# A fused attention and maxout kernel: unit 0's q and k in fp32 by Sync's queue, row maxima and crossbar transposes from unit 2 on, last two tiles as 64-row pairs, a new order table

## The chip, the cores and the metric

The kernel runs on one core of one Trainium2 chip. The metric is device time in microseconds (us) of one execution. Before the change three runs gave 293.11, 294.73 and 296.16 us, median 294.73. Profiles show one execution; its times count from the span's start.

## The reference

Inputs are `q`, `k`, `v` of shape (8 batches, 8 heads, 576 rows, 64), `w_phi` (64 x 128), three weights `w1`, `w2`, `w3` (512 x 768) and `w_out` (768 x 512), all float32. What is computed:

```python
def phi(x):
    proj = einsum('bhsd,df->bhsf', x, w_phi)
    proj = proj - max(abs(proj), axis=-1, keepdims=True)
    return concatenate([exp(proj), exp(-proj)], axis=-1)
q_p, k_p = phi(q), phi(k)
kv  = einsum('bhsf,bhsd->bhfd', k_p, v)
z   = sum(k_p, axis=2)
num = einsum('bhsf,bhfd->bhsd', q_p, kv)
den = einsum('bhsf,bhf->bhs', q_p, z)[..., None] + 1e-06
x   = (num / den) as (batch*row, head*dim)          # 4608 x 512
out = maximum(maximum(x @ w1, x @ w2), x @ w3) @ w_out
```

## The kernel before, in words

**Units.** Attention is cut into 16 units of four heads, half a batch each (`attention(u)`, L437 on). A unit's 4 x 576 rows stand as 18 tiles of 128 columns by two head pairs: tiles 0 to 8 and 9 to 17, of which 8 and 17 are "the last two tiles". In the work of one unit, by the letters that the code gives to its steps:

- L: q, k and v are loaded. For units 0 to 3 (`BY_PE`) POOL issues DMAs that cast q and k to bf16 on the way; only unit 0's k comes in fp32 by Sync's queue (`K0_SP`, L446 to L457), in two halves that VectorE casts. From unit 4 on q and k come in fp32 by Sync and GpSimd casts them.
- T: q and k are transposed, so that q has partitions 0 to 63 and k 64 to 127 of `qkT`: on TensorE for units 0 to 3 (L491), by one DMA crossbar transpose from unit 4 on (L506).
- G: the projections with `w_phi` (L521 to L534). Tiles in groups of four are done as 64-row matmuls, q and k as a pair of instructions side by side in the array (L533), into one PSUM bank each; the last two tiles as one 128-row matmul each, q and k side by side in 256 columns of one bank (L528). From unit 2 on (`JOIN`) two groups of four stand in one step.
- Maxima of the absolute values by VectorE (L552) and exponentials of k by ScalarE (L546).
- R, mT, V (from unit 4 on, `SUBT`): the maxima of q are transposed on TensorE (L560), copied, and written by a small DMA as row 64 of `qkT`, so that the second projection M subtracts them with a row of -1 in its weights (L613). For units 0 to 3 (`by_product`) M adds 34 small products with a negated identity instead (L618).
- K: `kv` from exponentials and scaled v, as 64-row matmuls (L642). N: the numerators and denominators (L660), divided by VectorE into `x_sb` (L666, L667).
- X: x is transposed into `xT`. For units 0 to 5 (`X_PE`) by ten TensorE transposes (L680) and two copies (L683), from unit 6 on by one DMA crossbar transpose on Sync's queue (L690).

**Chunks.** The second part runs by `chunk` (L697): eight chunks of 512 tokens, one for each batch, and a ninth of the 8 x 64 rows left over. `w1` is subtracted from `w2` and `w3`, and `w1 @ w_out` is made once (L814), so a chunk has 12 "up" steps of 4 matmuls (L713) and, for each of four row tiles, 4 matmuls with that product (L741) and 6 with `w_out` (L746), an evacuation (L754) and a store (L761). Chunk b needs the X steps of units 2b and 2b+1.

**Order.** Nothing is scheduled at run time. Every step is a node; the string `PLAN` lists, for each node, its number, its engine (T, D, A, G, S for PE, DVE, ACT, POOL, SP), the buffers that it gets, and a start time by which `fill` (L269) sorts the nodes. Each engine then runs its instructions in that order, and an engine whose next instruction waits lets nothing pass. Where `PLAN` leaves gaps on PE, `fill` puts matmuls without use ("idler", L846) that keep PE busy. There are eight PSUM banks, written out in `PLAN` too.

Of the kernel before, what the change touches and what calls it, by code (L numbers as in the profile page):

```python
# [16 lines left out]
DF = 128  # L17
# [24 lines left out]
X_PE = 6  # L42
SUBT = 4
# [3 lines left out]
JOIN = 2  # L47
# [4 lines left out]
K0_SP = 1  # L52
GATES = (None, (0, 0), (1, 0), (2, 0))
V_ACT = 4
# [48 lines left out]
47A0@17.5 63A@17.6 56A@18.1 54A@18.6 49G@14.6 45G@15.7 1054G@16.8 1062D0@14.4 46G@17.6 51G@18.7 50G@19.0 1052G@20.1
84D1@15.6 1066D@15.7 86T4@16.4 90T6@16.9 88T3@17.1 87D1@17.2 89D@17.8 91D@18.4 92T110211@18.0 102T41@18.6 97T35@18.8
112T6@19.1 95D@18.6 96D@19.3 107T70@19.4 103A@19.1 113A@19.6 93A@20.0 108A@20.5 109A@21.1 85S@15.8 105D@19.9 110D@20.5
67T047@21.2 115D@21.1 100D@21.4 106D@22.0 94A@21.6 98A@22.1 104A@22.8 68A@23.3 128T31@22.3 1063T2@22.8 222G0@20.9
159T1@23.4 131T4@24.0 129A@23.7 116D@22.6 69D@23.0 111D@23.3 121A1@24.2 114A@24.4 123G1@24.6 124G@25.7 101D@24.0
137T7@24.6 130A@24.7 139A@25.2 117A@25.6 99A@25.8 138A@26.3 118G@26.0 119G@27.1 122G@28.2 125T0@24.8 132A@26.6
133A@27.3 120A@27.8 134T6@25.3 136A@27.9 135A@28.6 126A@29.0 127A@29.7 223G@29.3 76T30@25.8 1053G@30.2 1057G@31.0
1055G@33.1 1064D@24.6 160D2@25.7 74T2@26.1 70T5@26.5 77D0@26.3 71D1@27.0 75D0@27.6 1071T1@26.8 157D2@28.3 1072D@28.4  # L110
158S@28.5 165T00735400@28.1 161T2@28.7 163T1@29.2 169D@29.0 164D@29.6 168D@29.8 172D@30.4 162D@31.0 166A@30.2
167A@30.8 1073T6@29.3 140T110@30.7 173D@31.6 174T7532@31.9 182D@32.6 1074A@31.3 141A@32.1 181D@33.2 177D@33.8
183T6@32.3 142A@32.5 185A@32.9 180A@33.3 179A@34.0 1069T1@32.7 170A@34.5 1070A@35.0 72T0@34.0 149T31@34.3 178D@34.4
187D@35.0 186D@35.5 188A0@35.5 175A@35.7 191A0@36.2 1067T7@34.6 190G@35.9 189G@38.0 1068A@36.4 1056G@40.1 150D1@35.8
143T2@35.9 80T1@36.2 147T3@36.6 145T7@37.0 144D0@36.5 224D3@37.1 73D1@37.2 146D0@37.8 148D1@38.4 225S@37.3 356S1@38.0
355S0@38.6 359G1@43.2 358G@44.7 201T20@37.4 176A@36.9 184A@37.4 195T5@37.8 192T6@38.3 171A@37.7 81D@39.0 202A@38.2
203A@38.8 290S0@40.3 151T0@38.8 78T4@39.1 153T7@39.4 152D@39.5 1060D@40.2 154D@40.8 79D@41.3 204T3@39.7 226T2@40.0
207T010@40.5 193A@39.3 205A@40.2 206A@40.7 197A@41.0 228T3@41.6 230T7@42.2 227D0@41.7 194A@41.5 196A@42.0 208A@42.5
198T4@42.3 209D@42.3 229D@42.7 232T11625011@42.9 1097T1@43.5 1085T3@44.4 199A@43.1 234A@43.7 231D@43.3 239D@43.7
236D@44.4 212T70@45.3 235D@45.0 233A@45.1 289S1@42.9 293G2@46.7 292G@49.1 1086A1@45.6 200A@46.1 213D0@45.9 360S1@46.0  # L120
1098D@46.5 237A@46.6 1081T5@45.6 250T6@46.5 241T2374@46.7 253D@47.1 244D@47.6 1058D@48.2 248D@48.8 1082A@47.1
247A@47.6 243A@48.1 252A@48.6 238A@48.9 1079T1@47.3 1080A@49.4 251A@49.9 1077T5@48.3 1083T2@49.1 242A@50.2 1078A@50.7
421S0@50.6 1084A@51.2 1089T7@50.0 249D@49.4 254D@50.4 240D@50.7 1090D@51.4 245D@52.0 1059D@52.6 265T11@50.9 262T6@51.4
271T5@51.8 273A@52.3 246A@52.7 272A@53.2 210T0@52.1 214T2@52.4 211D1@53.2 215D0@53.8 1087T7@52.7 1093T3@53.6
216T4@54.5 548S1@51.2 294S2@52.5 422S0@57.8 547S1@58.4 357S0@59.7 266A@53.5 263A@54.0 267A@54.5 268T5@54.8 218T0@55.3
255A1@55.0 264A@55.2 219A@55.8 1099T2@55.6 259T1@56.4 258A1@56.5 257G@55.4 256G@57.5 269A@56.6 260A@57.2 261A@57.8
270A@58.3 1094D@54.7 217D1@55.3 1088D@56.0 1100D@56.7 291S1@61.2 1397G@59.5 361T00364000@56.9 368D@57.7 364D@58.4
1095T7@57.5 1091T2@58.5 1096D@59.0 1092D@59.6 369D@60.2 370T1453@59.3 362A@58.8 375A@60.2 1101T7@59.9 367A@61.0
363A@61.5 379T2@60.9 378D@60.8 377D@61.4 382D@62.0 373D@62.4 381A@62.5 376A@62.9 365D@63.0 383D@63.6 374D@63.9
1102T@61.1 1105T5@62.4 1106T@63.3 384T1@64.6 1103A0@63.3 380A@64.1 274T136@64.6 1107D1@64.8 387A0@64.7 385A0@64.9  # L130
424G0@59.9 366A@65.2 390A0@65.7 550G1@66.5 425G@67.6 295T11721511@66.0 300A@66.7 297A@67.2 388G@68.7 389G@70.8
386S@65.3 275D@66.0 298D@66.7 276D@67.3 281T01@66.5 1109T3@67.0 296A@67.9 372A@68.4 301A@68.9 371A@69.3 283T7@67.9
279T6@68.2 282D0@67.7 284D1@68.4 280D0@69.1 1110T@68.5 1111A2@70.1 299D@69.7 1113T0@69.8 302D@70.3 303D@70.9
304T7642@70.7 305A@71.5 277T3@71.3 307D@71.5 278D1@72.1 311D@72.7 426S0@68.9 484S0@71.8 394T10@71.7 423S2@72.4
396A@72.2 395A@72.8 1114T@71.9 313T5@73.2 1115A3@73.5 220T7@73.4 287T3@73.7 611S0@73.7 610S1@75.2 486S3@76.6 317D@73.7
221D@74.0 308D@74.5 285T1@74.0 286A@74.6 310A@75.3 306A@75.7 288D@75.1 406T040@74.4 391T7@75.5 403T1@75.8 404A@76.2
309A@76.6 405A@77.1 407D@75.7 408D@76.1 312D@77.2 316D@77.8 1125T3@75.9 397T4@76.8 1119T6@77.0 1131T0@77.9 1120D0@78.2
399A@77.4 398A@78.0 392A@78.5 393A@79.2 315A@79.6 318T1@78.8 1132D@79.0 319D1@79.6 321A1@80.0 314A@80.2 324G1@80.4
320S@80.0 551G@80.7 1104S@80.7 411T20@78.8 487G2@81.8 1126A@80.6 1117T4@79.1 1129T6@80.0 1127T0@80.9 400T7@81.8
1118A@81.1 1128A@82.0 322G@82.9 323G@85.0 402A@82.5 401A@83.1 1130D@81.7 412D0@82.3 1139T1@82.0 1140D@83.1  # L140
436T00534600@82.8 1121T0@83.4 442A@83.7 441A@84.3 437A@84.8 438A@85.4 439D@83.7 443D@84.3 444D@84.9 427T2715@84.5
434D@85.5 440D@86.2 430D@86.8 433A@85.9 1122A@86.4 1123T4@85.1 1137T6@86.0 445T1@86.9 325T31@87.1 447A@87.4 326A@87.7
1124A@88.2 1135T0@87.4 1145T2@88.2 327A@88.7 448D@87.9 1138D@88.2 449D@88.8 446A@89.3 450T4@89.1 1133T6@89.2
1136D@89.2 451D0@89.8 331T3@90.0 328T1@90.2 432A@89.7 428A@90.2 429A@90.8 330A@91.3 435D@90.3 1134D@90.9 340T104@90.5
332A@91.8 341A@92.3 342D@91.9 431D@92.2 1149T5@91.6 1150T@92.6 1151D0@94.1 329A@92.7 453A0@93.1 333A@93.4 334T6@93.9
613G0@87.1 335A@94.3 336A@95.0 552S1@82.2 485S1@85.1 553T11407111@94.1 571T3@94.7 614G@88.2 575D@95.2 557D@95.6
560D@96.2 1146T@95.0 454G0@93.5 488G@95.6 574D@96.8 674S0@89.5 675S0@90.1 559A@95.5 558A@96.1 555A@96.6 556D@97.1
561D@97.7 572A@97.3 1108S@90.7 1116S@91.9 337T5@96.3 1141T6@96.4 1152S@94.9 549S1@96.1 1142T@97.3 1147A1@97.6
# [144 lines left out]
def kernel(  # L293
# [11 lines left out]
):  # L305
    nc = tc.nc

    try:
        from concourse.hw_specs import get_activation_tables
        _tables = list(get_activation_tables(nc.m.arch).keys())  # L310
        _set_id = _tables.index("natural_log_exp_and_others")
# [58 lines left out]
    def by_pairs(t):  # L370
        return t.rearrange("p (pr c) d -> p pr (c d)", c=NT)
# [506 lines left out]
```

## Time and profile before

| | |
|---|---|
| runs | 293.11, 294.73, 296.16 us |
| span of the profiled execution | 290.6 us |
| its whole time | not listed; the runs lie 2.5 to 5.6 us above the span |
| PE busy | 279.4 us, 3602 matmuls |
| DVE, ACT, POOL busy | 215.9, 189.9, 117.4 us |
| granted TensorE clock | 1.000 |
| HBM read, written | 34.67 MB, 9.44 MB |

The profile lists busy time for each engine; PE is matmuls, PEld loads of weights, which overlap them. A matmul's duration in a row is its way through the pipeline and not its price: the price is the step from its start to the next one's start. SPq, ACTq and POOLq rows are DMAs being issued. "DMA share" is the mean busy share of the 16 DMA engines; it is summed over packets and can pass 1.00 a little.

### The profile page before, as it was taken

How to read it: one execution, taken by the hardware profiler on the slowest of the kernel's cores; microseconds unless marked ns; L12 is line 12 of the kernel's file. 1: busy time of each engine (PE TensorE's matmuls, PEld its weight loads, DVE VectorE, ACT ScalarE, POOL GpSimd, SP SyncE). 2: the span in 40 equal slices, each digit the busy share in tenths (PEclk: the TensorE clock that was granted, in tenths of full speed). 3: DMA queues.
4: the chain of work that ended last, by engine and by line, in shares of the span. 5: the costliest groups of instructions: out<-in, count | busy, mean ns of one | idle time of the engine just before them, and what ended most of it. 6: DMA issues, size and time to landing. Idle time of an engine off the chain costs nothing.

```text
span 290.6 us, 8659 instructions
## 1 busy us (share of the span) xinstructions
PE 279.4 (96%) x3602; PEld 158.7 (55%) x3641; DVE 215.9 (74%) x457; ACT 189.9 (65%) x438; POOL 117.4 (40%) x101
## 2 busy tenths in 40 slices
PE   8878999999999999999999999999999999999993
PEld 3556685646645585564466556545555564444442
DVE  2987999998876899768989959898796583242360
ACT  1599798977988899799669797566858631120101
POOL 8086886276093751552780519107064300000000
PEclk9999999999999999999999999999999999999999
DMA  7999988997967799796995779658534523500605
GB/s 191 208 201 181 218 249 271 230 335 178 356 132 258 221 189 279 165 287 130 298 182 106 173 235 206 138 126 174 102 107 95 112 21 72 126 18 2 144 18 128
DMA packets 63051, 49.87 MB, mean 172 GB/s; under 512 B 43556, under 2 KB 48036, under 8 KB 63012
## 3 DMA queue, kind: packets, MB, share of 16 engines
q1 hardware_dynamic: 58644, 44.04, 61.2%
q0 software_dynamic: 4288, 5.21, 11.0%
q8 instruction: 28, 0.46, 0.6%
q14 instruction: 11, 0.09, 0.1%
q10 hardware_dynamic: 80, 0.07, 0.1%
HBM read 34.67 MB, written 9.44 MB: 152 GB/s over the span
## 4 chain that ended last, share of the span: by engine, by line
PE 86%; DVE 6%; ACT 4%; DMA 2%; issue 1%; SPq 0%; ACTq 0%
PE ups L713 30%; PE ops L746 16%; PE ops L741 11%; PE kvps L642 7%; PE psn L660 6%; PE psq L533 5%; PE psm L613 4%; DVE mqp L552 2%; DMA wphi_f<-in_w_phi_dram 2%; DVE mk L552 2%; ACT Ek L546 2%; PE tps L491 1%; PE pxT L680 1%; PE psm L618 1%; PE psq L528 1%
## 5 line engine op out<-in xcount | busy, mean ns | idle before, releaser
L588 POOL TENSOR_TENSOR vab<-v_raw,em 128x1152 bf16<-128x1152 f32 (+1 forms) x36 | 68.2, 1907 | 88.7 <-ACT em L584 67.7
L713 PE MATMUL ups<-xT,w_bf 128*128 128x512 bf16 x411 | 100.7, 379 | 1.1
L546 ACT ACTIVATE Ek<-psk 128x512 bf16<-128x512 f32 x128 | 70.5, 607 | 23.7 <-PE psk L533 17.0
L626 ACT ACTIVATE Eq<-psm 128x512 bf16<-128x512 f32 (+1 forms) x160 | 79.2, 586 | 7.9 <-PE psm L613 6.2
L713 PEld LDWEIGHTS <-w_bf 128*128 128x128 bf16 x432 | 40.3, 98 | 44.1 <-DVE x_sb L667 0.2
L746 PE MATMUL ops<-wout_bf,hT 128*128 128x512 bf16 (+1 forms) x219 | 50.7, 373 | 0.3
L552 DVE TENSOR_REDUCE mqp<-psq 128x4 bf16<-128x512 f32 (+1 forms) x80 | 47.7, 631 | 2.0 <-PE psk L533 1.0
L719 DVE TENSOR_TENSOR hT<-hT,ups 128x512 bf16<-128x512 bf16 x54 | 35.9, 683 | 14.2 <-ACT hT L721 6.8
L552 DVE TENSOR_REDUCE mk<-psk 128x4 f32<-128x512 f32 x64 | 42.5, 681 | 1.7 <-ACT Ek L546 1.2
L746 PEld LDWEIGHTS <-hT 128*128 128x128 bf16 x222 | 21.3, 98 | 22.8 <-DVE hT L719 0.2
L721 ACT ACTIVATE hT<-ups 128x512 bf16<-128x512 f32 x28 | 16.4, 613 | 26.2 <-PE ups L713 26.1
L667 DVE TENSOR_TENSOR x_sb<-psn,rden 128x320 bf16<-128x320 f32 x64 | 31.5, 492 | 2.2
L660 PEld LDWEIGHTS <-Eq 128*128 128x128 bf16 x640 | 24.5, 97 | 6.5 <-issue 0.3
L754 DVE COPY osb<-ops 128x512 f32<-128x512 f32 (+1 forms) x19 | 12.6, 674 | 18.9 <-PE ops L746 18.9
L660 PE MATMUL psn<-kv_sb,Eq 128*128 128x65 bf16 x640 | 26.3, 193 | 0.1
L723 DVE TENSOR_SCALAR hT<-ups 128x512 bf16<-128x512 f32 x26 | 17.5, 686 | 11.4 <-PE ups L713 11.1
L754 ACT COPY osb<-ops 128x512 f32<-128x512 f32 (+1 forms) x18 | 10.3, 575 | 23.7 <-DMA out_dram<-osb 9.6
L741 PE MATMUL ops<-xT 128*128 128x512 bf16 x86 | 24.1, 380 | 0.5
L642 PEld LDWEIGHTS <-Ek 64*128 64x128 bf16 x1152 | 18.4, 94 | 5.7 <-issue 2.8
L642 PE MATMUL kvps<-vab,Ek 64*128 64x65 bf16 x1152 | 20.5, 190 | 0.9 <-POOL vab L588 0.5
L533 PE MATMUL psq<-w,qkT 64*128 64x128 bf16 x256 | 20.4, 217 | 0.4 <-DVE qkT L494 0.4
L533 PEld LDWEIGHTS <-qkT 64*128 64x128 bf16 x512 | 14.5, 94 | 10.7 <-issue 7.7
(72 smaller groups left out, 277.8 us busy)
## 6 DMA issues: line engine op xcount, KB each, us to landing
v_raw<-in_v_dram SPq DMA_DIRECT2D x16, 576.0 KB, 4.6
out_dram<-osb SPq DMA_DIRECT2D x70, 128.0 KB, 2.4
k_raw<-in_k_dram SPq DMA_DIRECT2D x12, 576.0 KB, 4.9
q_raw<-in_q_dram SPq DMA_DIRECT2D x12, 576.0 KB, 6.1
w_bf<-in_moe_w_dram POOLq DMA_DIRECT2D x3, 768.0 KB, 10.0
qk_bf<-in_q_dram POOLq DMA_DIRECT2D x3, 288.0 KB, 10.6
qk_bf<-in_k_dram POOLq DMA_DIRECT2D x3, 288.0 KB, 11.1
wout_bf<-in_moe_w_out_dram POOLq DMA_DIRECT2D x1, 768.0 KB, 9.5
```

The source lines that it names most:

```text
L533: nc.tensor.matmul(ps()[:, i, :], lhsT=cols[r, :], rhs=w2[r, c, :], start=True, stop=True)
L546: nc.scalar.activation(Ek[s]()[:, tiles_of(t0, n), :], of(1), EXP, scale=1.0 - 2.0 * s)
L552: nc.vector.tensor_reduce((mq, mk)[c]()[:, tiles_of(t0, n)], of(c), AXX, ALU.max, apply_absolute_value=True)
L588: (nc.vector if n_.eng == "DVE" else nc.gpsimd).tensor_tensor(vab()[:, g, t0:t1, 0:D], vb()[:, t0:t1, :], em()[:, g, t0:t1].unsqueeze(2).t ...
L626: nc.scalar.activation(Eqb()[s][:, cols], psm()[:, 0:w], EXP, scale=1.0 - 2.0 * s)
L642: nc.tensor.matmul(kvps[ab]()[:, t // NT, g, :], lhsT=Ek[g]()[r, t, :], rhs=vab()[r, g, t, :], start=(t + g == 0), stop=(t == UT - 1 and g ...
L660: nc.tensor.matmul(psn()[:, c, :], lhsT=Eqb()[g][:, t0:t0 + P], rhs=kv()[:, pr, ab, g, :], start=(g == 0), stop=(g == 1))
L667: nc.vector.tensor_tensor(x_sb()[:, pr, :, ab, :], psn()[:, :, 0:D], rden().to_broadcast([P, 5, D]), ALU.mult)
L713: nc.tensor.matmul(ups(), lhsT=w_bf[i + 1][:, ct, j * P:(j + 1) * P], rhs=tokens_of(ct), start=(ct == 0), stop=(ct == CT - 1))
L719: nc.vector.tensor_tensor(hT()[:, j, :], hT()[:, j, :], ups(), ALU.max)
L741: nc.tensor.matmul(ops_()[:, 0:width], lhsT=tile_of(ct, tt), rhs=line_w[c_i > MOVE][:, ct, cols], start=(ct == 0), stop=False)
L746: nc.tensor.matmul(ops_()[:, 0:width], lhsT=hT()[:, j, tt * P:(tt + 1) * P], rhs=wout_bf[:, j, cols], start=False, stop=(j == JT - 1))
```

## The change

Six things are changed together.

1. Unit 0's q, too, is loaded in fp32 in halves by Sync's queue (before: by POOL's casting DMAs). Sync's queue now begins with q, k, q, k halves and then v; three of the four casts are on ScalarE, one is on VectorE.
2. `w_phi` is loaded by ScalarE's queue, ahead of ScalarE's table load (before: by Sync's queue after the k halves).
3. The maxima go as a row from unit 2 on (before: from unit 4), and x goes by crossbar from unit 2 on (before: from unit 6).
4. The last two tiles are projected as 64-row pairs into two banks, and no two groups of four are joined in one step.
5. The ninth chunk's stores have 128 rows in one DMA (before: two of 64 rows), and they may be issued by ScalarE; the row of maxima may, too.
6. `PLAN` is new throughout: every engine's order, every buffer and every bank.

Of the order, what the prediction uses, from the built programs: POOL's DMAs run k1, q1, w1, q2, k2, w_out, k3, w2, q3, w3, where the digit after q or k is the unit (before: q0 in two halves, w1, then q and k of units 1 and 2, with w_out after the first two products with v). The four new crossbar transposes stand on Sync's queue among the loads of units 7 to 10.

The main differences in the counts of the built programs:

```
PE   psm<-minus,mqp 128x64 / 128x128     128 / 8  ->  64 / 4
PE   pxT<-ident,x_sb 128x128                  60  ->  20
PE   psq<-w,qkT 128x256 (128 rows)            32  ->   0
PE   psq and psk<-w,qkT 128x128 (64 rows)    512  -> 576
PE   pmT<-ident,mqp 128x128                   12  ->  14
PE   idler 128x512                            23  ->  19
PE   changes between 64- and 128-row forms    97  -> 100
DVE  xT<-pxT copies                           10  ->   2
DVE  hT<-ups copies                           26  ->  18   (ACT 28 -> 36)
SP   DmaTranspose xT<-x_sb                    10  ->  14
SP, ACT  qkT<-mT                              12  ->  14
ACT  q and k casts of unit 0                   0  ->   3
POOL qk_bf<-in_q casts of unit 0               2  ->   0
SP   out_dram<-osb                            73  ->  67   (ACT 1 -> 2)
```

The diff, without the lines of `PLAN` and the functions that only moved:

```diff
-X_PE = 6
-SUBT = 4
+X_PE = 2
+SUBT = 2
...
-JOIN = 2
+JOIN = UNITS
...
-K0_SP = 1
-V_ACT = 4
...
+    queue_of = {"SP": nc.sync, "ACT": nc.scalar}
...
+    wphi_f = const.tile([P, DF], FP32, name="wphi_f")
+    for ab in range(2):
+        nc.scalar.dma_start(wphi_f[ab * D:(ab + 1) * D, :], w_phi)
...
-    def phi_load():
-        nc.sync.dma_start(wphi_f[0:D, :], w_phi)
-        nc.sync.dma_start(wphi_f[D:2 * D, :], w_phi)
...
-                    if u == 0 and what == 1 and K0_SP:
+                    if u == 0:
...
-                            nc.sync.dma_start(by_pairs(raw()[:, ts, :]), rows_of(1, 0, p0, p1))
+                            nc.sync.dma_start(by_pairs(raw()[:, ts, :]), rows_of(what, 0, p0, p1))
...
-                psq, psk = bank("psq", [P, 4, DF]), bank("psk", [P, 4, DF]) if n == 4 else None
+                psq, psk = bank("psq", [P, 4, DF]), bank("psk", [P, 4, DF])
...
-                        if n == 2:
-                            nc.tensor.matmul(psq()[:, 2 * i:2 * i + 2, :].rearrange("p a f -> p (a f)"), lhsT=cols,
-                                             rhs=w2.rearrange("p a f -> p (a f)"), start=True, stop=True)
-                            continue
                         for c, ps in enumerate((psq, psk)):
                             r = slice(c * D, (c + 1) * D)
                             nc.tensor.matmul(ps()[:, i, :], lhsT=cols[r, :], rhs=w2[r, c, :], start=True, stop=True)
...
-            on_act = u < V_ACT
-            n_v = nd("V", {"ACT" if on_act else "SP": 0.7}, lambda: (nc.scalar if on_act else nc.sync).dma_start(
-                qkT()[D:D + 1, :].rearrange("o (t c) -> o t c", c=P), mT()), [n_mt] + projs, [mT, qkT],
-                lat=2.2, pipe=0.0 if on_act else 0.1)
+            n_v = nd("V", {"ACT": 0.7, "SP": 0.7}, None, [n_mt] + projs, [mT, qkT], lat=2.2, pipe=0.1)
...
-          lambda tt: [(out[(2 * tt + i) * S:(2 * tt + i + 1) * S, :].rearrange("(i c) n -> c i n", c=NT)[NT - 1], slice(i * ST, (i + 1) * ST))
-                      for i in range(2)], 2)
+          lambda tt: [(out.rearrange("(r c) n -> c r n", c=NT)[NT - 1, tt * P:(tt + 1) * P], slice(0, P))], 1)
```

More of the change, by code (lines that the diff above doesn't have):

```diff
@@ L103 @@
[L103 to L112, printed above, removed]
@@ L244 @@
+1420S@270.6 1462T@269.6 1463A2@271.1 1464A@271.9 1469T1@270.9 1458T@271.3 1459D3@272.8 1460S@273.6 1465T2@272.6 1470T@273.1
+1471A0@273.9 1472S@274.5 1466T@273.7 1467A1@274.6 1468A@275.1
 """
@@ L373 @@
     wphi_f = const.tile([P, DF], FP32, name="wphi_f")
+    for ab in range(2):
+        nc.scalar.dma_start(wphi_f[ab * D:(ab + 1) * D, :], w_phi)
+    try:
+        from concourse.hw_specs import get_activation_tables
+        _tables = list(get_activation_tables(nc.m.arch).keys())
+        _set_id = _tables.index("natural_log_exp_and_others")
+    except Exception:
+        _set_id = 6
+    nc.scalar.add_instruction(
+        mybir.InstLoadActFuncSet(
+            act_func_set_id=_set_id,
+            name=nc.get_next_instruction_name(),
+            ins=[],
+            outs=[],
+        )
+    )
     ident = const.tile([P, P], BF16, name="ident")
@@ L415 @@
     n_const = node("const", 0, {"DVE": 2.2}, zeros, [n_idle], [])
-    n_phi = node("phi", 0, {"SP": 1.2}, phi_load, [], [], pipe=0.05, lat=2.0, dmas=2)
+    n_phi = node("phi", 0, {"ACT": 1.2}, lambda: None, [], [], pipe=0.05, lat=2.0, dmas=2)
     n_phi = node("phi", 0, {"DVE": 0.7}, phi_weights, [n_phi, n_const], [])
@@ L534, in attention @@
                 mms.append(proj)
-            tiles = [ps for x in given for ps in x[2:] if ps]
+            tiles = [ps for x in given for ps in x[2:]]
             ti = 2 if n == 2 else t0 // NT
-            a = nd("G", {"PE": 0.22 if n == 2 else 0.236 * len(part)}, lambda mms=mms: [f() for f in mms], [tr[ti], n_phi],
-                   [qkT, mk, mq] + tiles + Ek, mode=int(n == 4))
+            a = nd("G", {"PE": 0.12 if n == 2 else 0.236 * len(part)}, lambda mms=mms: [f() for f in mms], [tr[ti], n_phi],
+                   [qkT, mk, mq] + tiles + Ek, mode=1)
             projs.append(a)
@@ L542, in of @@
                 def of(c, n=n, psq=psq, psk=psk):
-                    return (psq, psk)[c]() if n == 4 else psq().rearrange("p (t c) f -> p t c f", c=2)[:, :, c, :]
+                    return (psq, psk)[c]()[:, 0:n, :]
                 def ex(s, t0=t0, n=n, of=of):
@@ L548, in attention @@
                     exps.append(nd("ek", {"ACT": 0.49 if n == 4 else 0.34}, lambda s=s, ex=ex: ex(s), [a],
-                                   [psk or psq, Ek[s]], locks=[psk or psq]))
+                                   [psk, Ek[s]], locks=[psk]))
                 for c in range(2):
@@ L553, in red @@
                                                 apply_absolute_value=True)
-                    ps = psk if c and psk else psq
+                    ps = (psq, psk)[c]
                     reds.append(nd("r", {"DVE": 0.607 if n == 4 else 0.34}, red, [a, n_const], [ps, (mq, mk)[c]], locks=[ps]))
```

317 lines of the change are left out of this document (152 added, 165 removed).

## The prediction

> **What bounds the kernel now.** I read the page's busy times first, then busy time by stage, then single rows.
>
> ```profile
> span 290.6 us, 8659 instructions
> PE 279.4 (96%) x3602; PEld 158.7 (55%) x3641; DVE 215.9 (74%) x457; ACT 189.9 (65%) x438; POOL 117.4 (40%) x101
> PEclk9999999999999999999999999999999999999999
> ```
>
> ```profile
> core 0: us, PE busy (x) PEld busy (x) DVE busy (x) ACT busy (x) POOL busy (x), PEclk, DMA share, GB/s
> 0.00:20.00 20.00, 17.44 (x209) 9.44 (x210) 13.36 (x36) 10.97 (x27) 10.60 (x20) 1.00 1.00 207
> 20.00:40.00 20.00, 18.06 (x407) 12.84 (x408) 17.88 (x43) 17.79 (x47) 15.44 (x15) 1.00 1.03 182
> ...
> 60.00:80.00 20.00, 19.78 (x321) 12.08 (x323) 17.62 (x38) 15.58 (x36) 8.19 (x7) 1.00 0.92 299
> 80.00:100.00 20.00, 19.84 (x212) 10.12 (x214) 14.98 (x30) 17.15 (x40) 15.23 (x12) 1.00 0.74 208
> 100.00:120.00 20.00, 19.84 (x360) 12.72 (x362) 18.71 (x46) 17.71 (x42) 4.72 (x5) 1.00 0.91 203
> 120.00:140.00 20.00, 19.84 (x247) 10.98 (x249) 15.25 (x32) 17.64 (x41) 11.21 (x8) 1.00 0.90 224
> 140.00:160.00 20.00, 19.79 (x304) 11.75 (x308) 17.52 (x39) 14.53 (x34) 9.33 (x8) 1.00 0.80 183
> ```
>
> The first column after the window is PE. From 60 us on it is busy 19.8 of every 20 us at full clock: there TensorE is the bound, and work taken from it counts one for one as long as nothing else is late. Ahead of 40 us it is not full, and there the DMA share is 1.00 and 1.03: the first 40 us are bound by the bytes that units 0 to 3 and the weights need. So a stage bound by transfers is followed by one bound by TensorE, in which the DMA engines are 74 to 92% busy. That second number is what the change will lean on.
>
> **TensorE's work, step by step.** The price of a matmul is the step to the next start. I take it from the order of time on PE, in two stretches.
>
> ```profile
> 55.88 0.40 PE L618 MATMUL psm<-minus,mqp 128*128 128x64 bf16 x8
> 56.12 0.44 PE L680 MATMUL pxT<-ident,x_sb 128*128 128x128 bf16 x5
> 56.40 1.03 PE L713 MATMUL ups<-xT,w_bf 128*128 128x512 bf16 x4
> ```
>
> ```profile
> 57.48 0.40 PE L618 MATMUL psm<-minus,mqp 128*128 128x64 bf16 x8
> 57.80 0.23 PE L533 MATMUL psq<-w,qkT 64*128 64x128 bf16 x1
> ...
> 58.21 0.22 PE L533 MATMUL psk<-w,qkT 64*128 64x128 bf16 x1
> 58.36 1.90 PE L713 MATMUL ups<-xT,w_bf 128*128 128x512 bf16 x7
> ...
> 61.62 0.38 PE L528 MATMUL psq<-w,qkT 128*128 128x256 bf16 x2
> 61.84 1.46 PE L746 MATMUL ops<-wout_bf,hT 128*128 128x512 bf16 x6
> ```
>
> Eight subtractions take 56.12 - 55.88 = 0.24 us, five transposes 56.40 - 56.12 = 0.28. The last two tiles take 61.84 - 61.62 = 0.22 as 128-row matmuls. Eight 64-row pairs start between 57.80 and 58.21, seven steps of 0.059. Going into the 64-row form costs 57.80 - 57.48 - 0.24 = 0.08, going out 58.36 - 58.21 - 0.06 = 0.09.
>
> - Units 2 and 3 lose 8 groups of eight subtractions (1.9 us) and four 128 wide at a transpose's 0.056 (0.2): -2.1. The first product of each M step stays at the same size, with other weights. Two more transposes of the maxima: +0.1.
> - Units 2 to 5 lose 8 groups of five transposes: -2.2.
> - 16 units project the last two tiles in two pairs, 0.12 instead of 0.22: -1.6.
> - Joined groups are dissolved, but the built order puts groups side by side: 97 changes of form become 100, +0.3.
>
> Sum on TensorE: -5.5 us. Fewer idlers change nothing; they stand only in waits. Each of these edits counts only while TensorE is the bound; if it waits for something else, they count 0.
>
> **The last stores.**
>
> ```profile
> 281.41 6.80 SPq L761 DMA_DIRECT2D out_dram<-osb  x9
> 281.41 0.56 ACTq L761 DMA_DIRECT2D out_dram<-osb  x1
> ...
> 285.98 0.37 ACT L754 COPY osb<-ops 128x256 f32<-128x256 f32 x1 [1.84 <-PE ops L746]
> ```
>
> Nine issues stand in a row on Sync's queue until 288.21; the last copy is done at 286.35. With half as many, divided over two queues, the last issue follows its copy: 286.35 + 0.56 = 286.9, 1.3 us sooner, and the 2.4 us from there to the end stay. -1.3. The bounds are 0 (a single longer DMA lands later) and -1.3.
>
> **The first 40 us.**
>
> ```profile
> 1.43 1.29 POOL L460 DMA_DIRECT2D qk_bf<-in_q_dram  x2
> ...
> 3.65 0.70 DVE L453 CAST qk_bf<-k_raw 128x576 bf16<-128x576 f32 x1 [1.66 <-DMA k_raw<-in_k_dram]
> ```
>
> ```profile
> 6.70 0.80 PE L491 MATMUL tps<-ident,qk_bf 128*64 128x128 bf16 x16
> ...
> 7.88 0.23 DVE L403 CAST w<-wphi_f 64x128 bf16<-64x128 f32 x1 [1.64 <-DMA wphi_f<-in_w_phi_dram]
> 8.12 0.22 DVE L404 CAST wphi_m<-wphi_f 64x128 bf16<-64x128 f32 x1
> 8.27 0.45 DVE L453 CAST qk_bf<-k_raw 128x576 bf16<-128x576 f32 x1
> 8.40 0.61 PE L491 MATMUL tps<-ident,qk_bf 128*64 128x128 bf16 x5
> ```
>
> k's half by Sync is there at 3.65; the first transposes wait until 6.70 for q. The second cast of k stands on VectorE behind the cast of `w_phi`, which landed at 7.88. Both waits go: q's half follows k's on the same queue, and ScalarE casts it. Late next are the second halves and the weights. Four halves then share the DMA engines with POOL's transfers, in which k1 takes q0's place at 1.43 and w_out stands ahead of unit 3's q and k. The bytes needed until TensorE is full stay the same, and the DMA share over these 40 us is 1.0 already. A start that is 1 to 2 us earlier therefore only moves the wait to a later place. I take 0. Bounds: -4.0, nearly all of the 2.6 + 1.9 us that TensorE lacks in the first two windows; and +3.0, a wait like the 6.70 - 3.65 above, moved to w_out.
>
> **The crossbar and the rows of maxima.**
>
> ```profile
> v_raw<-in_v_dram SPq DMA_DIRECT2D x16, 576.0 KB, 4.6
> ...
> q_raw<-in_q_dram SPq DMA_DIRECT2D x12, 576.0 KB, 6.1
> ...
> qkT<-qk_bf SPq DMA_TRANSPOSE x12, 8.3
> ...
> xT<-x_sb SPq DMA_TRANSPOSE x10, 4.2
> ```
>
> ```profile
> 236.00:244.00 8.00, 7.95 (x62) 4.16 (x63) 5.75 (x15) 0.75 (x2) 0.40 (x1) 1.00 0.59 84
> ...
> 60.00:100.00 40.00, 39.62 (x531) 22.20 (x536) 32.61 (x66) 32.73 (x74) 23.42 (x19) 1.00 0.83 253
> ```
>
> In 236 to 244 us two crossbar transposes of x run with next to nothing beside them: 8 x 0.59 / 2 = 2.4 us of all 16 engines each. Four more make 9.4 us, in a stage (60 to 100) that has 40 x 0.17 = 6.8 us free. They and the loads behind them on Sync's queue get late by some 2.6 us, and the stages behind have room to catch up (0.80 at 140 to 160). Who waits is the chunk that needs this x, and with it all of PE. What used to hide a late load, 5.5 us of TensorE's own work, is smaller too. I take +2.0, near the 2.6 of this one stage, since some chunks have more slack than that. Bounds: 0 and +11 (the third rival). The two new rows of maxima are of 4.5 KB; no wait of PE for such a row is in the trace, so 0; if the steps between are not filled with other work, one row costs its issue and landing, at the nearest the 2.4 us of a small store.
>
> Off the path: VectorE loses 8 copies and gains none, ScalarE gains three casts and eight evacuations, with 35% of its time idle; the second bank of the last two tiles is 0 as long as PE finds a free bank, as it does now for all but 0.2 us in 20.
>
> **Sum.** 290.6 - 5.5 - 1.3 + 0 + 2.0 = 285.8 us of span, -4.8. The runs shown have a median of 294.73, 4.1 above the span; the same 4.8 from it gives 289.9 us.
>
> [...]
>
> **Rivals.**
>
> 1. The crossbar is as cheap as a load. The stage from 60 to 100 moves 253 GB/s at 0.83, so 305 GB/s when full; 0.33 MB of x are then 1.1 us, four are 4.3, which fit into 6.8, and nothing is late: 287.9 us. Against it stands the 0.59 of the row above.
> 2. The pairs stand alone. If each unit's last two tiles were an excursion of their own, 16 x 0.17 = 2.7 us are paid for the 1.6 saved: 292.6 us. The built order, with three more changes of form in all, speaks against it.
> 3. The DMA engines become the bound (the case on the other side). In 60 to 160 us they work 18.4 + 14.8 + 18.2 + 18.0 + 16.0 = 85.4 us. With 9.4 more it is 94.8, in a stage that TensorE would pass in about 94.5. That needs a share of 1.00, which the trace shows only for the loads of the first 40 us; in the stages with many crossbar transposes it shows 0.90 and 0.91. At 0.90 the stage takes 105.3 us, 11 later: 290.6 - 6.8 + 11 + 4.1 = 298.9 us. It decides from a share below 94.8 / 101.3 = 0.94 on.
> 4. The start wins. If what is won in the first 10 us is kept, -4.0: 285.9 us.
> 5. The start loses. Halves in fp32 arrive no sooner than the casting DMAs did, or w_out is late: +3.0, 292.9 us.
>
> **How the numbers follow.** A measurement of this kernel can tell about 1%, 2.9 us, from no change; faster is below 291.8, slower above 297.7. The forecast, 289.9 with its own range of 287 to 293, has 0.40; rival 1 0.12, rival 2 0.04, rival 3 0.20, rival 4 0.14, rival 5 0.10. Faster: 0.34 of the forecast's 0.40, 0.12 and 0.14, sum 0.60. Same: the rest of the forecast 0.06, rivals 2 and 5 with 0.14, a third of rival 3: 0.27. Slower: the rest, 0.13. The range goes from 284 (rival 4 with a little of rival 1) to 298 (most of rival 3).
>
> **What would show it.** Right: PE busy falls to about 273, no subtraction rows but units 0's and 1's, 32 fewer 256-wide rows; PE reaches 19.8 in 20 us at about the same 40 us; the end stands about 3.5 us after the last matmul. Steps are wrong if the stages behind 60 us show PE below 19.5 in 20 with a wait for `xT` or `qkT` by DMA (rival 3), if PE is full before 36 us (rival 4), or if the first transposes come later than 6.7 (rival 5). The prediction is wrong if the DMA share stays below 0.94 while PE waits.

## The result, and the profile after

The changed kernel takes 291.05 us in the median of 18 runs (288.70 to 293.66), the kernel before 293.76 in 18 runs beside them (292.11 to 296.18). The ratio is 0.9887, with a 95% interval of 0.9859 to 0.9915: 3.3 us faster (2.5 to 4.1), at the bound of 1% that the prediction set itself. The prediction said 289.9, and 4.8 us faster. Ratios, here and below, leave out the runs that lie over 1.5% above the fastest of their kernel, which leaves three of the six runs of the experiment e7, whose profile belongs to one of the others.

The two profiled executions stand differently to their medians. The span of 290.1 us below belongs to a run of 291.96 us, 0.9 above the median; the runs listed with their span lie some 1.8 us above it, so the 290.6 us of the kernel before belong to about 292.4, 1.4 below its median. So 0.5 us between the spans and 2.7 between the medians are no contradiction, and single spans are read here only for where time lies.

The page of the changed kernel; a digit of the clock's line is a fortieth of the span:

```profile
span 290.1 us, 8530 instructions
...
PE 274.1 (94%) x3526; PEld 154.6 (53%) x3563; DVE 203.6 (70%) x433; ACT 199.4 (69%) x455; POOL 117.2 (40%) x102
...
PEclk9897999999999999999999999999999999999999
```

PE's busy time is 5.3 us less than before (279.4; 1.1 of it are idlers, 7.70 us instead of 8.79), and yet the span is only 0.5 less: PE stood idle for 16.0 us where it was 11.2. Where, is seen by stage: first the changed kernel to 40 us, then from 40 to 160 us, with the sum of these six stages, then two rows of the same view of the kernel before. PE's busy time is the number behind the stage's length; the last three are clock, DMA share and GB/s:

```profile
core 0: us, PE busy (x) PEld busy (x) DVE busy (x) ACT busy (x) POOL busy (x), PEclk, DMA share, GB/s
0.00:20.00 20.00, 14.57 (x158) 7.19 (x158) 11.41 (x32) 11.39 (x23) 7.96 (x16) 0.91 0.97 236
20.00:40.00 20.00, 18.82 (x413) 13.78 (x416) 16.80 (x35) 17.08 (x43) 14.15 (x17) 0.91 1.14 242
```

```profile
40.00:60.00 20.00, 18.61 (x259) 10.84 (x259) 18.47 (x39) 16.93 (x42) 13.68 (x10) 1.00 0.83 214
60.00:80.00 20.00, 19.23 (x339) 11.73 (x341) 18.29 (x41) 18.48 (x44) 14.80 (x11) 1.00 1.10 243
80.00:100.00 20.00, 19.08 (x290) 10.48 (x292) 17.37 (x37) 18.65 (x42) 9.81 (x8) 1.00 0.97 224
100.00:120.00 20.00, 18.61 (x288) 11.00 (x286) 16.45 (x39) 15.64 (x37) 10.99 (x9) 1.00 0.99 248
120.00:140.00 20.00, 19.75 (x324) 11.68 (x323) 16.42 (x37) 16.36 (x38) 9.75 (x7) 1.00 1.08 254
140.00:160.00 20.00, 19.81 (x277) 11.35 (x274) 17.55 (x38) 16.10 (x40) 10.76 (x10) 1.00 1.04 226
sum 120.00, PE 115.08 PEld 67.06 DVE 104.55 ACT 102.17 POOL 69.80; mean PE 19.18 PEld 11.18 DVE 17.43 ACT 17.03 POOL 11.63
```

```profile
40.00:60.00 20.00, 19.79 (x317) 12.75 (x317) 18.71 (x38) 17.69 (x40) 12.66 (x8) 1.00 0.98 264
...
sum 120.00, PE 118.88 PEld 70.39 DVE 102.80 ACT 100.31 POOL 61.34; mean PE 19.81 PEld 11.73 DVE 17.13 ACT 16.72 POOL 10.22
```

Before (the last fence), PE was full from 40 us on. Now four stages of 20 us in a row, 40 to 120, show 18.61 to 19.23: 118.88 - 115.08 = 3.8 us of PE are lost there. Ahead of 40 us, PE is busy for 33.40 us instead of 17.44 + 18.06 = 35.50, so 2.1 are lost there too, of which the 1.1 of the idlers are work without use. What PE waited for in the whole span (line, releaser, sum, number, longest), and the three longest pieces of the chain of waits that are transfers:

```profile
PE tps L483 <- ACT qk_bf L445: 2.5, 2, 1.3
PE pwT L783 <- DMA w_bf<-in_moe_w_dram: 1.8, 1, 1.8
PE ups L700 <- DMA xT<-x_sb: 1.2, 1, 1.2
...
PE pxT L667 <- DVE x_sb L654: 0.9, 1, 0.9
PE psm L600 <- DVE hT L706: 0.8, 1, 0.8
...
PE psm L600 <- DMA qkT<-mT: 0.6, 1, 0.6
```

```profile
3.57 16.96 DMA w_bf<-in_moe_w_dram
66.42 4.74 DMA qkT<-mT
104.45 7.08 DMA xT<-x_sb
```

Three transfers stand on the chain: `w1`, 17 us from its issue until PE goes on, a row of maxima of 4.5 KB, 4.7 us, and the x of one unit by crossbar, 7.1 us. The kernel before had none of the three among its waits of PE. But of the 3.8 us between 40 and 120, only the 0.6 and the 1.2 are put down to transfers. The 0.9 (in 40 to 60 us) and the 0.8 (in 80 to 100) are put down to VectorE, which came late with `x_sb` and with `hT`, and 0.3 to nothing that the profile shows. The start and the end of the span (start, duration, engine, line; what ended the wait stands in brackets), and below them the last matmuls of the kernel before:

```profile
5.43 0.64 PE L483 MATMUL tps<-ident,qk_bf 128*64 128x128 bf16 x16
...
9.43 0.24 PE L483 MATMUL tps<-ident,qk_bf 128*64 128x128 bf16 x1 [1.15 <-ACT qk_bf L445]
...
10.98 0.69 PE L483 MATMUL tps<-ident,qk_bf 128*64 128x128 bf16 x17 [1.31 <-ACT qk_bf L445]
```

```profile
285.25 1.47 PE L733 MATMUL ops<-wout_bf,hT 128*128 128x256 bf16 x12
...
286.76 0.37 ACT L741 COPY osb<-ops 128x256 f32<-128x256 f32 x1 [0.28 <-PE ops L733]
```

```profile
285.08 0.82 PE L746 MATMUL ops<-wout_bf,hT 128*128 128x256 bf16 x6
```

The first transposes start at 5.43 instead of 6.70, and then PE waits 1.15 and 1.31 us for ScalarE's casts of the second halves. The last matmul ends at 286.72, 3.4 us ahead of the end (before: 285.90, 4.7 ahead), so the last stores give 1.3 us.

### The profile page after: what moved, and what is told of

Read it like the earlier page. It is cut to its first block, busy times and chain, and to the rows that moved or that the text cites. A ratio compares the mean times of both kernels' runs of the same rounds, so it can differ in the third digit from the quotient of the medians.

```text
span 290.1 us, 8530 instructions
## 1 busy us (share of the span) xinstructions
PE 274.1 (94%) x3526; PEld 154.6 (53%) x3563; DVE 203.6 (70%) x433; ACT 199.4 (69%) x455; POOL 117.2 (40%) x102
## 4 chain that ended last, share of the span: by engine, by line
PE 84%; DMA 10%; DVE 3%; issue 1%; POOL 1%; ACT 0%; POOLq 0%; DVEq 0%
PE ups L700 32%; PE ops L733 15%; PE ops L728 9%; PE psn L647 6%; PE kvps L629 6%; DMA w_bf<-in_moe_w_dram 6%; PE psq L521 5%; PE psm L600 5%; DMA xT<-x_sb 2%; DMA qkT<-mT 2%; PE pm L797 1%; PE tps L483 1%; DVE x_sb L654 1%; PE psm L602 1%; POOL qk_bf L452 1%
## 5 line engine op out<-in xcount | busy, mean ns | idle before, releaser
L534 ACT ACTIVATE Ek<-psk 128x512 bf16<-128x512 f32 (+1 forms) x160 | 81.6, 567 | 13.3 <-PE psk L521 6.9
L540 DVE TENSOR_REDUCE mk<-psk 128x4 f32<-128x512 f32 (+1 forms) x80 | 49.3, 630 | 3.1 <-PE psk L521 1.7
L741 ACT COPY osb<-ops 128x512 f32<-128x512 f32 (+1 forms) x24 | 13.7, 578 | 33.9 <-PE ops L733 27.4
L733 PEld LDWEIGHTS <-hT 128*128 128x128 bf16 x222 | 21.0, 98 | 22.1
L708 ACT ACTIVATE hT<-ups 128x512 bf16<-128x512 f32 x36 | 21.7, 609 | 14.5 <-PE ups L700 13.6
L521 PE MATMUL psq<-w,qkT 64*128 64x128 bf16 x288 | 25.3, 223 | 1.4 <-DVE qkT L486 0.7
L521 PE MATMUL psk<-w,qkT 64*128 64x128 bf16 x288 | 25.3, 224 | 0.0
L521 PEld LDWEIGHTS <-qkT 64*128 64x128 bf16 x576 | 17.1, 96 | 14.0 <-issue 10.4
L600 PE MATMUL psm<-qkT,wphi_m 128*128 128x512 bf16 (+1 forms) x70 | 21.7, 358 | 1.4 <-DVE hT L706 0.8
L741 DVE COPY osb<-ops 128x512 f32<-128x512 f32 x13 | 8.9, 686 | 18.9 <-PE ops L733 16.1
L469 POOL CAST qk_bf<-k_raw 128x1152 bf16<-128x1152 f32 x12 | 14.1, 1185 | 18.2 <-DMA k_raw<-in_k_dram 13.0
```

The source lines that it names most:

```text
L521: nc.tensor.matmul(ps()[:, i, :], lhsT=cols[r, :], rhs=w2[r, c, :], start=True, stop=True)
L534: nc.scalar.activation(Ek[s]()[:, tiles_of(t0, n), :], of(1), EXP, scale=1.0 - 2.0 * s)
L540: nc.vector.tensor_reduce((mq, mk)[c]()[:, tiles_of(t0, n)], of(c), AXX, ALU.max, apply_absolute_value=True)
L600: nc.tensor.matmul(psm()[:, 0:w], lhsT=wphi_m, rhs=rhs, start=True, stop=True)
L733: nc.tensor.matmul(ops_()[:, 0:width], lhsT=hT()[:, j, tt * P:(tt + 1) * P], rhs=wout_bf[:, j, cols], start=False, stop=(j == JT - 1))
```

## The experiments

The theory after this reading: TensorE's work and the end are worth the 6.8 us that the prediction summed; the start is worth nothing; and some 4 us are given back between 40 and 120 us, where transfers come too late for a TensorE that now gets to them sooner. Its rivals: that the work taken from TensorE counts for less, since other engines set the pace; that the four crossbar transposes or the queue of the rows of maxima cost the time; that the order of the new table does; that the clock does (the 9897 above). Ratios are to the kernel before on the same chip, with 95% intervals. The first four ran on one chip, so did e5 to e8, e9 to e11, and e12.

**The changed kernel again.** No edit.

> The changed kernel once more, beside which the others of this call are read. Theory (transfers): 0.985 to 0.992 of before; PE again waits for the late halves of q and k near 8 to 11 us, for w1 near 19, and for rows of maxima and crossbar transposes between 40 and 115 us, and the granted clock is again halved for two stretches of 3.4 us in the first 26 us, as PE has just been idle ahead of each. Rival (chance): the halved clock was that one execution's; here it is 1.0 throughout and the span some 2 us shorter.

Measured: 0.9915 (0.9880 to 0.9949), 291.50 us; span 287.7. PE has 116.25 us between 40 and 160, 2.6 fewer than before, and nearly all that it waits for there are two rows of maxima:

```profile
PE psm L600 <- DMA qkT<-mT: 2.5, 2, 1.3
```

`w1` is late again ahead of 28 us, for 1.5 us. Which transfer is late changes from one execution to the next (here none for x); that some are late in that stage does not.

**Idlers into the gaps of the first 20 us.** More products without use, against a low clock. The edit puts in twenty, not the fourteen of the expectation, since the lines ahead of the transposes are run for q and for k: the profile has 39 idlers, the changed kernel's 19.

```diff
+                            if u == 0 and nb == 2 and n == 1:
+                                for _ in range(6):
+                                    product(0)()
...
         def turn(g=g, pwT=pwT):
+            for _ in range(8 if g == 0 else 0):
+                product(0)()
```

> The changed kernel with 14 more products without use on PE: six ahead of the last transpose of unit 0's tiles 8 and 17, which waits for k's second half, and eight ahead of the first transposes of w1. If the halved clock comes from PE's idle time, the clock is 1.0 after both places and the first 30 us of work are up to 2.5 us shorter: 1 to 2.5 us below the changed kernel. If the transfers set the pace there anyway, 0 to 0.5 us below it.

Measured: 1.0083 (1.0042 to 1.0123), 295.87 us, slower than before and 1.7% slower than e1. The granted clock is 1.00 throughout, where the changed kernel had 0.60 from 12 to 16 us (the number ahead of the DMA share; the first fence). But the twelve idlers of the first place hold PE for twice 2.5 us (the second fence), and the transposes of the second halves start at 13.85 instead of 10.98:

```profile
8.00:12.00 4.00, 1.54 (x35) 1.15 (x32) 1.28 (x3) 2.33 (x4) 0.00 (x0) 0.97 1.12 281
12.00:16.00 4.00, 3.93 (x35) 1.50 (x32) 3.71 (x8) 3.42 (x8) 0.70 (x1) 0.60 1.11 281
```

```profile
8.71 2.55 PE L420 MATMUL idler<-idle 128*128 128x512 bf16 x6
...
11.37 2.55 PE L420 MATMUL idler<-idle 128*128 128x512 bf16 x6
13.85 0.69 PE L492 MATMUL tps<-ident,qk_bf 128*64 128x128 bf16 x17
```

So the idlers took more than the full clock gave, and this run does not settle what the clock is worth. e9 does, for the 4 us in question.

**x of units 2 to 5 by a plain DMA.** The crossbar's mode alone is taken away, so these x are not transposed; the bytes, the place and the queue stay.

```diff
             def xdma():
+                if u < 6:
+                    nc.sync.dma_start(xT[:, b, ct0:ct0 + 2, :], x_sb().rearrange("p q t a d -> p q (t a d)"))
+                    return
```

> In units 2 to 5 the crossbar transpose of x is a plain DMA of the same bytes on the same queue, so the transposition of these x is left out. Theory (the crossbar's small packets make later transfers late): PE's waits at 70 to 115 us shrink by 1.5 to 3 us, and the time with them. Rival (the loads moved ahead and the order itself make them late): within 0.5 us of the changed kernel, the same waits.

Measured: 0.9887 (0.9843 to 0.9931), 290.24 us; against e1 0.3% less, within the intervals. The transfers did get cheaper. The traces have a landing time for one of the four alone, the second: 2.7 us by plain DMA, 3.4 by crossbar in the changed kernel. To issue, the four hold Sync's queue for 0.48 to 0.55 us each, where the crossbar's held it for 1.34 to 1.36 and once for 2.08. Rows of this kernel first, then of the changed one:

```profile
xT<-x_sb SPq DMA_DIRECT2D x1, 320.0 KB, 2.7
```

```profile
98.84 0.51 SPq L678 DMA_DIRECT2D xT<-x_sb  x1
```

```profile
xT<-x_sb SPq DMA_TRANSPOSE x1, 3.4
```

```profile
99.75 1.36 SPq L677 DMA_TRANSPOSE xT<-x_sb  x1
```

Neither moved the time by what can be measured; PE's sum from 40 to 160 us is 116.06, among the others of the changed kernel, with a new wait of 1.7 us for q and k by crossbar. The crossbar as the whole cause falls; the two intervals leave room for a part of it, up to some 2.5 us.

**The last two tiles as 128-row matmuls.** The order and the two banks stay as changed.

```diff
                             r = slice(c * D, (c + 1) * D)
+                            if n == 2:
+                                r = slice(0, P)
```

> The last two tiles of each unit projected by 128-row matmuls again, q and k in two banks, so four steps of 0.056 us a unit instead of two pairs. Theory (PE is the bound from 45 us on): 16 x 0.10 = 1.6 us more, and some 0.5 for six more changes of form, 2.1 in all. Rival (PE has waits enough to hide it): 0 to 0.5 us more.

Measured: 0.9963 (0.9929 to 0.9998), 292.65 us: 0.0048 above e1, 1.4 us, uncertain by about as much. That fits the 1.6 us that the prediction gave to the pairs, and would just allow nothing; the loss of its second rival is out.

**All rows of maxima on ScalarE's queue.**

```diff
+        if n.kind == "V":
+            n.eng = "ACT"
         n.end = n.start + n.costs[n.eng] + LATENCY[n.eng]
```

> The changed kernel with every row of maxima issued on ScalarE's queue; in the changed kernel the planner chose between Sync's and ScalarE's, and the rows of units 2 to 6 that stand behind loads on Sync's land 4 to 5 us after their issue. Nothing else is moved. Theory (TensorE's saving is given back by transfers that land late, the row of maxima among them): the waits for qkT<-mT at 71 and 96 us go, 1.0 to 1.8 us in all, the ratio falls by 0.003 to 0.006 to about 0.984. Rival (the row is late because the DMA engines are full, whatever queue it stands on): the same waits, ratio within 0.003 of the changed kernel's. Second rival (ScalarE's issues stand ahead of its evacuations and hold PE up): 0 to 1 us slower.

Measured: 0.9882 (0.9825 to 0.9939), 290.76 us, span 289.0. PE's waits for `qkT<-mT` are gone, but others stand in their place, one of them for VectorE, and PE has 18.76 of 20 us from 40 to 60 and 18.85 from 100 to 120:

```profile
PE pxT L669 <- DVE qkT L488: 1.0, 1, 1.0
PE ups L702 <- DMA xT<-x_sb: 0.9, 1, 0.9
```

Against the changed kernel's 0.9887 and 0.9915 no gain is shown.

**Unit 5's load later.** On Sync's queue one load of 0.56 MB goes behind unit 2's, so that `w1` has less beside it. The edit is one entry of a line of `PLAN`.

```diff
-360S1@17.2
+360S1@25.8
```

> The changed kernel with one load of 0.56 MB for unit 5, which no step needs before 45 us, moved on Sync's queue from 17 to 26 us, behind unit 2's. Theory (the first 40 us lose what the start won, since w1 lands late among loads that nobody needs yet): w1 lands about 1.5 us earlier, the wait of PE at 18.6 falls from 1.6 to 1.9 to near 0, and the time by 1 to 1.5 us, ratio about 0.985. Rival (what the DMA engines owe by 40 us stays the same, so a wait only moves): the wait at 18.6 goes, PE has the same sum at 40 us, ratio within 0.003 of the changed kernel's.

Measured: 0.9859 (0.9808 to 0.9911), 289.55 us, span 287.7. The wait for `w1` falls to 0.8 us, and two for rows of maxima take 2.2:

```profile
PE psm L600 <- DMA qkT<-mT: 2.2, 2, 1.5
...
PE pwT L783 <- DMA w_bf<-in_moe_w_dram: 0.8, 1, 0.8
```

The lowest median of the kernels that do all the work. Its interval holds the 0.9887 of the changed kernel and ends just short of the 0.9915 of e1, and the intervals overlap, so a gain is not shown.

**Unit 0's q by POOL's casting transfers again.**

```diff
-                            nc.sync.dma_start(by_pairs(raw()[:, ts, :]), rows_of(what, 0, p0, p1))
+                            if what == 0:
+                                nc.gpsimd.dma_start(by_pairs(qk()[:, 0, ts, :]), rows_of(0, 0, p0, p1))
+                            else:
+                                nc.sync.dma_start(by_pairs(raw()[:, ts, :]), rows_of(what, 0, p0, p1))
...
```

> The changed kernel with the two halves of unit 0's q by POOL's casting transfers again, and without ScalarE's casts of them; k's halves stay on Sync's queue, the rest as it is. Theory (the start as changed is worth little: the first transposes 1.3 us earlier, then waits of 1.3 and 1.4 us for the second halves and 1.6 to 1.9 for w1): the first transposes at 6.5 or later, and the end within 1.5 us of the changed kernel's, 0 to 0.5 % slower. Rival (the fp32 halves crowd the others out and cost 2 us): faster than the changed kernel by 1 us or more. Second rival (the start's gain is kept): slower by the full 1.3 us or more.

Measured: 0.9849 (0.9773 to 0.9924), not told apart from the changed kernel; all six runs have a median of 291.81. The first transposes start at 6.63, the waits for casts are gone, and three rows of maxima alone cost 3.3 us:

```profile
PE psm L604 <- DMA qkT<-mT: 3.3, 3, 2.5
PE tps L487 <- DMA qk_bf<-in_q_dram: 1.2, 2, 0.7
```

What the start is worth cannot be seen while a later wait takes up what it wins. Hence e12.

**The kernel before without 68 subtractions.**

```diff
-                nc.tensor.matmul(psm()[:, 0:w], lhsT=w2[:, 0, :], rhs=rhs, start=True, stop=False)
+                nc.tensor.matmul(psm()[:, 0:w], lhsT=w2[:, 0, :], rhs=rhs, start=True, stop=u > 1)
+                if u > 1:
+                    return
```

> The kernel before with the 68 subtracting matmuls of units 2 and 3 left out (those maxima are then not taken off), and nothing put in their place: no row, no wait. It asks what work taken from TensorE is worth where no transfer takes it back. Theory (TensorE is the bound behind 28 us, and the saving is real): 2.1 us less, ratio about 0.993. Rival (a chain beside TensorE, of maxima, exponentials and evacuations, sets the pace, so that the work counts for less): 0 to 0.7 us less, ratio 0.998 to 1.0.

Measured: 0.9951 (0.9924 to 0.9978), 292.31 us: 1.4 us less (0.6 to 2.2), where 2.1 were expected. The rival's 0 to 0.7 is nearly out: TensorE's work counts there, for two thirds of its price by this figure and for a third to all of it by the interval.

**Half the bytes of the later loads.** Units 4 to 15 read half of q, k and v and use it twice; no engine's work changes, but the result is that of the half.

```diff
...
+                m = 1 if u >= 4 else 2
...
-                    by_pairs(raw()), rows_of(what, u, 0, 2)), gates, [raw],
+                    by_pairs(raw())[:, 0:m, :], rows_of(what, u, 0, m)), gates, [raw],
...
-                qk()[:, :, c * D:(c + 1) * D], raw_bufs(u)[c]()), [mains[c]], [(qb, kb)[c], qk])
+                twice(qk()[:, :, c * D:(c + 1) * D]), first(raw_bufs(u)[c]())), [mains[c]], [(qb, kb)[c], qk])
...
```

> The changed kernel with half the bytes in each load of q, k and v of units 4 to 15: only the first of a unit's two pairs of heads is read, and every step that uses the tile uses that half twice, so all engines keep their instructions and sizes (the second pair's results are the first's). Some 10 MB less; between 40 and 115 us the DMA engines have about a fifth less to move, while the first 26 us stay as they are. Theory (what PE waits for between 40 and 120 us comes from DMA engines without room): the waits for rows of maxima and for x there fall from 3 to 5 us to under 1.5, and the time by 2 to 4 us, ratio 0.975 to 0.982. Rival (those waits come from the order of the queues and the steps, not from the bytes): within 0.003 of the changed kernel's 0.9887 to 0.9915.

Measured: 0.9748 (0.9709 to 0.9787), 286.14 us. All that PE waits for, and its sum from 40 to 160 us:

```profile
PE tps L490 <- ACT qk_bf L451: 2.7, 2, 1.4
PE pwT L795 <- DMA w_bf<-in_moe_w_dram: 2.2, 1, 2.2
PE idler L840 <- DVE idle L412: 1.0, 1, 1.0
PE pm L809 <- issue: 0.2, 1, 0.2
PE ops L745 <- issue: 0.2, 1, 0.2
```

```profile
sum 120.00, PE 118.71 PEld 69.12 DVE 108.10 ACT 105.93 POOL 73.38; mean PE 19.79 PEld 11.52 DVE 18.02 ACT 17.66 POOL 12.23
```

The waits of the start are the same, and no wait for a transfer is left behind the one for `w1`. PE is as full as in the kernel before. The order, the queues, the rows and the crossbars are all as changed: by themselves they cost PE no wait there. The granted clock is 0.91 in both of the first two stages of 20 us, as in the changed kernel, so the clock is not what the time between the two comes from.

**The same halves in the kernel before.** The edit of e9.

> The same halves in the kernel before: q, k and v of units 4 to 15 with the first pair of heads read alone and used twice. There PE waits for no transfer behind 28 us. Theory: 0 to 0.5 us less, ratio 0.998 to 1.0. Rival (the bytes cost something else as well, such as slower accesses of the engines to SBUF while transfers land): as much less as in the changed kernel, ratio 0.99 or below.

Measured: 0.9997 (0.9961 to 1.0033), 293.63 us. The bytes cost the kernel before nothing that is measured, within 1.1 us, so the 0.0139 between e9 and the changed kernel, 4.1 us (2.7 to 5.5, from both intervals), is what the bytes cost the changed kernel. That this comes by late transfers is read from the waits. In the changed kernel's trace half of the lost time stands directly behind transfers and the other half behind VectorE; with half the bytes both go, and how the bytes hold VectorE up is not shown. This execution has 117.21 us of PE between 40 and 160, so single profiles of the kernel before and of this variant differ by 1.7 us there; the nine profiles of the changed kernel and of its variants with full loads lie at 114.3 to 116.6.

**e5 and e6 together.** Both edits.

> The two single moves on the changed kernel together: unit 5's load behind unit 2's on Sync's queue, and all rows of maxima issued on ScalarE's queue. Alone they measured 0.9859 and 0.9882 against 0.9887 and 0.9915 of the changed kernel. Theory (each takes a wait of its own): 1.5 to 2.5 us less than the changed kernel, ratio 0.981 to 0.985. Rival (a wait taken away comes back at the next late transfer): 0.985 to 0.989, no better than either alone.

Measured: 0.9899 (0.9853 to 0.9946), 290.72 us, no better than either. That is what the rival expected of the time. Its reason, the next late transfer, is not in the trace: from 28 to 160 us PE waits for no transfer that the profile names. It stands 1.94 us in the middle of a row of projections, for nothing that the profile shows, with a DMA share of 0.16, and 1.0 us for VectorE's copy of `qkT`; then the clock is low:

```profile
PE psq L523 <- issue: 1.9, 1, 1.9
```

```profile
44.00:48.00 4.00, 2.01 (x48) 1.19 (x42) 2.99 (x4) 1.80 (x6) 4.00 (x4) 0.96 0.16 58
48.00:52.00 4.00, 4.00 (x23) 1.57 (x22) 3.16 (x7) 2.84 (x6) 3.15 (x3) 0.61 1.20 158
```

What held PE up there stays open. None of the moves that were tried makes a version that is shown to beat the changed kernel.

**e9 with e7.** Halved loads, and unit 0's q by POOL; no later wait can hide what q's way is worth.

> The kernel with halved loads of units 4 to 15 (half the bytes of q, k and v, the half in place used twice), in which PE waits for nothing behind 28 us, now with the two halves of unit 0's q by POOL's casting transfers again. Behind 28 us no late transfer can hide what the start is worth here. Theory (Sync's fp32 halves of q win 1.3 us at the first transposes and lose as much by waits of 1.3 and 1.4 us for the second casts and 2 us for w1): within 1 us of the kernel with halved loads, ratio 0.972 to 0.978 against its 0.9748. Rival (the start as changed costs about 2 us): ratio 0.967 to 0.970. Second rival (the gain of the first transposes is kept): ratio 0.979 or above.

Measured: 0.9736 (0.9687 to 0.9784), 286.72 us, against 0.9748 of e9: q's new way is worth nothing, in either direction, within about 1.8 us. `w_phi` and POOL's order stay as changed here, so this is not the whole start.

## Why the prediction was right, and where its sum was off

The time lies in the range, also in the forecast's own, 287 to 293. Step by step:

- **TensorE -5.5, last stores -1.3: right; first 40 us 0: fits, but is not shown singly.** Together -6.8. With the loads halved, e9 shows -0.0252 x 293.8 = -7.4 us (-8.5 to -6.3), which leaves -0.6 (-1.7 to 0.5) for the start if the other two have their price. Singly, the stores are 1.3 in the trace, the subtractions 1.4 (0.6 to 2.2) in e8 for 2.1, the pairs 1.4 for 1.6 in e4, uncertain by as much, and q's way 0 within 1.8 in e12. Against the 0 stands that PE is busy 2.1 us less ahead of 40 us, 1.0 without the idlers. That the first transposes come sooner, and the wait only moves, to the second halves and `w1`, was the forecast's reason, and the rows at 9.43 and 10.98 and the 17 us of `w1` show it. Its sign "PE reaches 19.8 in 20 us at about the same 40 us" is not kept: 18.61 from 40 to 60. That belongs to the next step.
- **The crossbar and the rows of maxima, +2.0: mis-sized, and put on the wrong edits.** What the transfers take back measured +4.1 (2.7 to 5.5). The step took a DMA share of 0.83 over 40 us as 6.8 us of room, and made the time late by the 2.6 us that four crossbars need beyond it. e3 takes their mode away and shows no gain; e5 takes the rows off Sync's queue, and other waits take their place; e9 takes bytes of loads that were not changed at all, and every wait behind `w1` but two of 0.2 us goes. What fits this is in a sentence of that step by the way: TensorE's own work "used to hide a late load". Nearly the same bytes are now needed in less time.
- **Rows of maxima at 0: wrong as a term of its own.** The 4.74 us of a 4.5 KB row stand on the chain, and e1, e6 and e7 wait 2.2 to 3.3 us for such rows. The price that was kept for that case, "the 2.4 us of a small store", is half of the 4.74.
- **Rival 3** (the DMA engines become the bound) has its sign, PE at 19.23, 19.08 and 18.61 behind 60 us with waits for `xT` and `qkT`, and about a third of its price of 11. The point from which it was to decide, a share below 0.94, told nothing: PE lost as much at 0.83 from 40 to 60 us as at 0.99 from 100 to 120. By the forecast's last sign, "the DMA share stays below 0.94 while PE waits", it would be wrong for the first of these; the waits there are put down to VectorE and to nothing shown, not to a transfer. The share is summed over packets and stood at 1.14 from 20 to 40 us, so 1 less the share is not shown to be free time. The outcome lies between the forecast and this rival.
- **Rival 1** (crossbar as cheap as a load, nothing late) named a cost that e3 cannot find, but its "nothing is late" did not come. **Rival 2** is out by e4. **Rivals 4 and 5** are out at their full size, -4.0 and +3.0, by e12 for q's way and by the -0.6 above for the whole start.

Part of the nearness is luck. The 289.9 starts from three runs with a median of 294.73; from the 293.76 of all 18 the same forecast is 289.0, 2.1 below what was measured.

Not settled: what held PE up in e11, how the bytes hold VectorE up, why PE's waits begin with so little less time for the loads (28.2 MB from 40 to 160 us by the rows of after, 27.6 by those of before), and whether the 1.3 MB of x or the time that PE no longer spends weighs more. An experiment that gives the kernel before a TensorE quicker by 5 us with no new transfer would tell; e8 was such a one for 2.1 us, and it brought 1.4.

## What to carry to other kernels

When work is taken from the engine that is the bound, ask first what that work was hiding: here 7 us were won and 4 given back, and the 4 stayed away when the loads were halved. What a DMA share of 0.83 leaves open was no room to plan with; halving the bytes of untouched loads in both kernels measures in one comparison what they cost. Where one wait is taken away and the time stays, look for the next wait before looking for another cause of the first.

## What the runs showed of the hardware

**The granted clock fell after idle times of 1.15 to 1.94 us, but not after every one.** In the changed kernel PE is busy 1.54 us of the 4 from 8 to 12 us, and the clock is 0.60 over the next 4; in e11 it is busy 2.01 of the 4 from 44 to 48, after 1.94 us of idle time in one piece, and the clock is 0.61 over the next 4. In e1 it stays at 1.00 from 16 to 32 us, with a wait of 1.5 for `w1`. In the order of time the steps of 64-row matmuls go from 0.06 to 0.11 us:

```profile
7.77 0.22 PE L521 MATMUL psq<-w,qkT 64*128 64x128 bf16 x1
...
7.83 0.22 PE L521 MATMUL psq<-w,qkT 64*128 64x128 bf16 x1
...
12.86 0.31 PE L521 MATMUL psq<-w,qkT 64*128 64x128 bf16 x1
...
12.97 0.31 PE L521 MATMUL psq<-w,qkT 64*128 64x128 bf16 x1
```

Over 12 to 15 us alone the changed kernel's clock is 0.50, which agrees with the steps, and over 22.1 to 25.1 us it is 0.50 again. The two waits before the first drop were 1.15 and 1.31 us with a matmul between them; the one before the second was 1.75 us, for `w1`.

**The crossbar transposes of x were dearer than plain DMAs of the same bytes at the same place**, to issue (1.34 to 2.08 us against 0.48 to 0.55, four each, 320 KB) and to land (3.4 us against 2.7, one each). In this kernel the difference was not what counted: e3 has the ratio 0.9887, the changed kernel 0.9887 and 0.9915. The medians to landing that the prediction and the pages give rest on few transfers: the 8.3 us on two of twelve (8.0 and 8.7), and the changed kernel's median for x on two of fourteen (3.4 and 6.7).
